# Fetching the sampled value blocks of sparse attention by SP's DMAs with register addresses, in place of GpSimd's indirect DMAs, for some of the sets

## The chip, the cores and the metric

The kernel runs on one core of one Trainium2 chip. The time is that of one execution on the device, in microseconds; the kernel before was timed three times, and the median counts. A profile of one further execution gives what every engine did and when.

## The reference

Block-sparse attention is followed by a feed-forward network. Attention has 4 batches, 8 heads, 768 positions and a head size of 64. Positions are grouped into 24 blocks of 32. A query block sees its neighbours, the first and the last block, and three sampled key blocks, which are an input and are the same for all batches and heads; the first and the last query block see everything.

```python
mask = np.abs(blk_i - blk_j) <= window          # window = 1
mask = mask | (blk_i == 0) | (blk_j == 0) | (blk_i == n_blocks - 1) | (blk_j == n_blocks - 1)
for qb in range(n_blocks):
    for kb in sampled_blocks[qb]:
        mask[qb*block:(qb+1)*block, kb*block:(kb+1)*block] = True
scores = np.where(mask, scores, -1e9)
attn = softmax(scores)
x = (attn @ v).transpose(0, 2, 1, 3).reshape(3072, 512)
h = x @ w_in                                     # 512 x 2048
g = np.maximum(h, 0.0) + np.log1p(np.exp(-np.abs(h)))
return g @ w_out                                 # 2048 x 512
```

The weights come as 64-bit floating point numbers, which the kernel turns into 32-bit ones itself.

## The kernel before

**Sets and units.** The 22 inner query blocks of a batch are taken four at a time: five groups of four and a last one of two. With the first and the last block, which see all keys and make a "whole" set of their own ahead of the last group, a batch has 7 sets, and the kernel 28: 0 to 4 are the groups of the first batch, 5 its whole set, 6 its last group of two blocks, 7 the first group of the next batch, and so on. A set is worked in two units of four heads each. A unit has scores (TensorE, L834), their masked minimum on VectorE (L840), exponents on ScalarE (L890), transposes on TensorE (L903) with a copy out of PSUM (L908, L910), and the product with the values (TensorE, L946; L960 for the whole sets, L933 for the last groups). After both units the set is normalised (L973 to L975), turned (L989) and put into the FFN's input (L1004, L1008). Units run as a pipeline: `pieces(n)` emits the scores of unit n + 2, the transposes of unit n + 1 and the products of unit n.

**Keys and values of a set.** Each of the four query blocks has eight key blocks: three neighbours, the first, three sampled, the last. The keys of the whole batch lie in SBUF; sampled ones are copied within SBUF by GpSimd (L715), at an address that comes from a register. The registers are loaded from a small packed table `pk` (L656), in which one 32-bit word holds the three samples of two query blocks, five bits each; `pack_blocks` makes it on VectorE (L579 to L585). The values are fetched from HBM for every set, into one of two buffers (`vbuf[m % 2]`, tile vg): the neighbours by one DMA from SP of 96 rows for each block (L755), first and last block by SP too (L764, L767), and the sampled ones by GpSimd's indirect DMA, one for each query block (L773), which fetches 96 rows of 2 KB after a column of row numbers in the table `ix`. `make_index` computes `ix` on VectorE for all four batches (L588 to L598). The buffer of set m + 2 comes free when the products of set m are done; `load_values(m + 2)` stands right behind them.

**What sets the order.** SP's instructions run in the order in which the program issues them: besides the value loads these are queries (`load_queries`, L649), key blocks of the next batch (L633), raw weights (L159) and converted weights on their way to HBM (L212), attention results (L1011) and output (L506, L512, L523). An instruction that waits holds back all behind it. GpSimd's indirect DMAs and key copies are kept in two lists, `value_work` and `key_work`, and `gather()` takes one of each after every piece of attention; `gathered(work, m)` empties a list up to set m before what needs it. GpSimd also does one step of the weight conversion (L193) and, in the second half, additions of the FFN (L337, L471). VectorE's order at the start is written out by hand: index, packed table, mask, key copies of set 0 (the `manual_schedule` block near L1079).

**Around it.** While the first sets run, TensorE has nothing else to do; a row of warm-up matmuls (L1077) stands ahead. From about 69 us on the FFN's matmuls (L268 to L270, L495 to L497) are mixed in. Attention ends at about 432 us, and the rest is FFN.

Of the kernel before, what the change touches and what calls it, by code (L numbers as in the profile page):

```python
# [8 lines left out]
F32 = mybir.dt.float32  # L9
# [10 lines left out]
BLOCK = 32  # L20
# [22 lines left out]
START = 4  # L43

SPREAD = 2

PARK = 8

# [9 lines left out]
def sparse_attention_ffn(  # L58
# [22 lines left out]
    nc = tc.nc  # L81
    B, NG, P, NP, NI, _ = q.shape
    NB = k.shape[2]
    S = NB * BLOCK
    LAST = NB - 1
# [7 lines left out]
    NR = 3  # L93
# [438 lines left out]
    ac = actx.enter_context(tc.tile_pool(name="ac", bufs=1, side="right"))  # L532
# [3 lines left out]
    blk = ac.tile([P, NB * NR * 2], I32, name="blk")  # L536
    rf = ac.tile([P, NB, NR], F32, name="rf")
# [3 lines left out]
    io = ac.tile([NR * BLOCK, 1], I32, name="io")  # L541
    first = ac.tile([P, 1], I32, name="first")
    iof = ac.tile([NR * BLOCK, 1], F32, name="iof")
    ixf = ac.tile([NR * BLOCK, NB], F32, name="ixf")
    ix = ac.tile([NR * BLOCK, B, NB], I32, name="ix")
    mask = ac.tile([P, NG, NS], F32, name="mask")
    iu = ac.tile([P, NG], I32, name="iu")
# [12 lines left out]
    for rows in (slice(0, NR * BLOCK), slice(NR * BLOCK, P)):  # L560
# [4 lines left out]
        out=vbuf[0][:, 0, 0, :], out_offset=None, in_=v,  # L565
# [11 lines left out]
    def pack_blocks():  # L577

        nc.vector.scalar_tensor_tensor(  # L579
            out=pkf, in0=rf[0:1, :, 1], scalar=32.0, in1=rf[0:1, :, 0], op0=ALU.mult, op1=ALU.add  # L580
        )
        nc.vector.scalar_tensor_tensor(
            out=pkf, in0=rf[0:1, :, 2], scalar=1024.0, in1=pkf, op0=ALU.mult, op1=ALU.add
        )
        nc.vector.tensor_copy(out=pk, in_=pkf[:, 1 : NB - 1])  # L585

    def make_index():
        nc.vector.tensor_copy(out=iof, in_=io)  # L588
        nc.vector.tensor_copy(out=rf, in_=blk.rearrange("p (i s w) -> p i s w", s=NR, w=2)[:, :, :, 0])

        for s in range(NR):
            rows = slice(s * BLOCK, (s + 1) * BLOCK)
            nc.vector.tensor_scalar(
                out=ixf[rows], in0=rf[rows, :, s], scalar1=float(BLOCK), scalar2=iof[rows, 0:1],
                op0=ALU.mult, op1=ALU.add,
            )
        for b in range(B):
            nc.vector.tensor_scalar_add(out=ix[:, b], in0=ixf, scalar1=float(b * S))  # L598

    def make_mask():  # L600
        nc.vector.tensor_copy(out=iuf, in_=iu)
# [36 lines left out]
    def overlapping(src, lo, n, rows):  # L638

        at = src[lo : lo + rows]  # L640
        pattern = [list(x) for x in at.ap]
        return bass.AP(at.tensor, at.offset, [pattern[0], [BLOCK * pattern[0][0], n], pattern[1]])

    def load_queries(m):
        if m >= len(order):
            return
        b, g = order[m]
        qc[b, g] = wk.tile([P, NP, NI, BLOCK], F32, tag="qc", name=f"qc{b}_{g}", bufs=2)
        nc.sync.dma_start(out=qc[b, g], in_=q[b, g])  # L649
# [3 lines left out]
    def registers(eng, us):  # L653
        for u in us:
            if (eng, u) not in regs:
                regs[eng, u] = eng.value_load(pk32[0:1, u : u + 1], min_val=0, max_val=(1 << 31) - 1)  # L656
        return [regs[eng, u] for u in us]
# [9 lines left out]
    def gathered(work, m):  # L667
        while work and work[0][0] <= m:
            work.pop(0)[1]()

    wanted = []

    def load_keys(*ms):

        wanted.extend(m for m in ms if m < len(order))
        while wanted and order[wanted[0]][0] in kT:
            gather_keys(wanted.pop(0))

    def end_keys(m, copies):

        for copy, slot, blkno in zip(copies, (NR, 2 * NR + 1), (0, LAST)):
            ins = copy(
                out=kg[m % 2][:, :, slot, :],
                in_=kT[order[m][0]][:, blkno : blkno + 1, :].to_broadcast([P, NI, NP * BLOCK]),
            )
            if m >= NG:
                tc.keep_in_program_order(ins)

    def gather_keys(m):
        b, g = order[m]  # L690
        ni = NI if g < NG - 1 else 2
        kd = kg[m % 2]

        def of_block(i):

            eng = (nc.vector if i < 2 else nc.scalar) if m == 0 else nc.gpsimd
            copy = nc.scalar.copy if m == 0 and i >= 2 else eng.tensor_copy
            if i == 0:
                at = kT[b][:, 4 * g : 4 * g + NR, :]
                pattern = [list(x) for x in at.ap]  # L700
                ins = nc.vector.tensor_copy(
                    out=kd[:, 0:ni, 0:NR, :].rearrange("p i s f -> p i (s f)"),
                    in_=bass.AP(at.tensor, at.offset, [pattern[0], [NP * BLOCK, ni], [1, NR * NP * BLOCK]]),
                )
                tc.keep_in_program_order(ins)
            if m % NG < 2 and i == (m >= NG):
                first = nc.vector.tensor_copy if m == 0 else nc.scalar.copy
                end_keys(m, (first, nc.scalar.copy))
            (r,) = registers(eng, [2 * g + i // 2])
            for s in range(NR):  # L710
                x = nc.s_assert_within(
                    eng.snap((r >> (16 * (i % 2) + 5 * s)) & 31), 0, LAST,
                    skip_runtime_bounds_check_because="a sampled block is one of the key blocks",
                )
                copy(  # L715
                    out=kd[:, i, 1 + NR + s, :], in_=kT[b][:, bass.ds(x, 1), :].rearrange("p n f -> p (n f)")
                )

        if g == 0 and b > 0:
            key_work.extend((m, lambda: None) for _ in range(ARRIVAL))  # L720
        key_work.extend((m, lambda i=i: of_block(i)) for i in range(ni))


# [15 lines left out]
    def load_values(m):  # L739
        if m >= len(sets):  # L740
            return
        b, g, whole = sets[m]
        vd = vg[sets[m]] = vbuf[m % 2]
        if whole:
            rows = vd.rearrange("p c i f -> p (c i) f")
            for n in range(0, NCH, 2):
                lo = b * S + n * P
                nc.sync.dma_start(
                    out=rows[:, n : n + 2], in_=v[lo : lo + 2 * P].rearrange("(t p) f -> p t f", p=P)
                )  # L750
            return
        ni = NI if g < NG - 1 else 2

        i0 = 1 if m == 0 else 0
        nc.sync.dma_start(  # L755
            out=vd[0 : 3 * BLOCK, 0, i0:ni], in_=overlapping(v, b * S + (4 * g + i0) * BLOCK, ni - i0, 3 * BLOCK)
        )
        if g < 2:

            for c, lo in enumerate((b * S, (b + 1) * S - BLOCK)):  # L760
                i1 = i0 if c == 0 else 0
                if m < SPREAD:
                    if i1 == 0:
                        nc.sync.dma_start(out=vd[3 * BLOCK : P, c, 0], in_=v[lo : lo + BLOCK])  # L764
                    spread.append((vd[3 * BLOCK : P, c, 0:1], vd[3 * BLOCK : P, c, 1:]))
                    continue
                nc.sync.dma_start(  # L767
                    out=vd[3 * BLOCK : P, c, i1:],
                    in_=v[lo : lo + BLOCK].unsqueeze(1).to_broadcast([BLOCK, NI - i1, DM]),
                )  # L770

        def of_block(i):
            nc.gpsimd.indirect_dma_start(  # L773
                out=vd[0 : 3 * BLOCK, 1, i, :],
                out_offset=None,
                in_=v,
                in_offset=bass.IndirectOffsetOnAxis(ap=ix[:, b, 4 * g + 1 + i : 4 * g + 2 + i], axis=0),
            )

        value_work.extend((m, lambda i=i: of_block(i)) for i in range(ni))  # L780


# [230 lines left out]
    def pieces(n):  # L1013
# [24 lines left out]
        def value_piece():  # L1038
            if n + 2 < len(units):
                exponents(n + 2)  # L1040
            if ended[1] is not None:
                turn(ended[1])
            if n < len(units):
                values(n)
                if ended[2] is not None:
                    load_values(ended[2] + 2)
            if scored is not None:
                load_queries(scored + 2)
# [27 lines left out]
    for n in range(WARM):  # L1076
        nc.tensor.matmul(warm[:, n % 4], ident, ident, start=True, stop=True)  # L1077
    with tc.manual_schedule(engines={mybir.EngineType.DVE}):
        make_index()  # L1079
        pack_blocks()  # L1080
        make_mask()
        load_keys(0)
        gathered(key_work, 0)
    load_queries(1)
    load_values(0)
    load_keys(1)
    scores(0)
    nc.vector.tensor_copy(out=mask[2 * BLOCK : P, NG - 1], in_=mask[0 : 2 * BLOCK, NG - 1])
    with tc.manual_schedule(engines={mybir.EngineType.Pool}):
        gathered(value_work, 0)  # L1090
        gathered(key_work, 1)
    spread_ends()
    load_values(1)
    load_keys(2)
    scores(1)
# [145 lines left out]
```

## Time and profile before

| | |
|---|---|
| median of three timed runs | 805.41 us (805.35 to 809.15) |
| profiled execution, its own time | 807.66 us |
| its span, first to last instruction | 805.6 us |
| TensorE busy | 767.6 us (95%) |
| VectorE, ScalarE, GpSimd busy | 597.4, 563.4, 397.2 us |
| mean granted TensorE clock | 0.979 |
| indirect DMAs (L773) | 88, 87.9 us of GpSimd, 998 ns on average |
| value loads from SP (L755, L764, L767, L748) | 24, 3, 12 and 12 |

The profile names engines PE (TensorE matmul), PEld (its weight loads), DVE (VectorE), ACT (ScalarE), POOL (GpSimd) and SP (SyncE); an added q is the engine's own queue of small instructions and DMA issues. A row of a timeline reads: start, duration, engine, line, operation, output tile <- input tiles, shape, number of instructions merged; in square brackets the idle time of the engine just before, and what ended it ("issue": nothing that the profile shows). A row of waits reads: who waited for whom, total time, number of waits, the longest. A row with a slash-separated triple gives the shortest, median and longest duration in ns.

### The profile page before, as it was taken

The numbers are of one execution on the slowest core, as the hardware profiler recorded it, in microseconds if no ns is written. First come the engines' busy times: TensorE is split into PE (matmuls) and PEld (weight loads), VectorE is DVE, ScalarE is ACT, GpSimd is POOL, SyncE is SP. The second block draws the span as 40 slices with busy tenths as digits, with TensorE's granted clock in tenths as the row PEclk, the third lists the DMA queues.
The fourth block names the chain that finished last, engine by engine and source line by source line (L and its number), as shares of the span: only waits on it lengthen the run. The fifth ranks groups of instructions, "written<-read, shape, count | busy, mean of one in ns | idle before, by whom it ended". The sixth has DMA issues, their size and how long they took to land.

```text
span 805.6 us, 21589 instructions
## 1 busy us (share of the span) xinstructions
PE 767.6 (95%) x8188; PEld 622.6 (77%) x8188; DVE 597.4 (74%) x1292; ACT 563.4 (70%) x1235; POOL 397.2 (49%) x617
## 2 busy tenths in 40 slices
PE   8688889999899999999999999999999999999997
PEld 8456657777677778777788878888998888988785
DVE  5667898887777777777655657888688797886654
ACT  4767877877687777777665767677776767766552
POOL 6663695543456426455100005425489597695400
PEclk9779998999999999999999999999999999999999
DMA  8669898678697786965714686221302315020021
GB/s 246 214 186 309 256 228 268 189 252 269 183 260 223 242 274 209 256 200 161 246 43 154 218 265 212 68 96 48 105 27 80 104 39 172 12 78 16 27 79 52
DMA packets 61175, 132.27 MB, mean 164 GB/s; under 512 B 5712, under 2 KB 18128, under 8 KB 60048
## 3 DMA queue, kind: packets, MB, share of 16 engines
q1 hardware_dynamic: 55072, 112.41, 44.6%
q0 software_dynamic: 5712, 17.57, 7.6%
q8 instruction: 64, 1.05, 0.6%
q10 hardware_dynamic: 288, 0.93, 0.3%
q14 instruction: 39, 0.32, 0.1%
HBM read 100.47 MB, written 30.41 MB: 162 GB/s over the span
## 4 chain that ended last, share of the span: by engine, by line
PE 55%; DVE 14%; ACT 14%; POOL 8%; issue 4%; DMA 2%; another core or an unknown queue 1%; POOLq 1%; SPq 0%; DVEq 0%; ACTq 0%
PE h L268 8%; PE h L269 7%; PE h L270 7%; PE o L495 5%; ACT pr L890 5%; PE o L496 5%; PE o L497 5%; PE t L903 3%; PE x L946 3%; POOL gq L337 3%; PE s L834 3%; DVE e L285 3%; POOL y L471 2%; PE acc L442 2%; PE acc L441 2%
## 5 line engine op out<-in xcount | busy, mean ns | idle before, releaser
L285 DVE SCALAR_TENSOR_TENSOR e<-u,e 128x512 f32<-128x512 f32 (+1 forms) x108 | 86.1, 797 | 94.4 <-ACT u L283 90.3
L337 POOL TENSOR_TENSOR gq<-gq 128x128 f32<-128x128 f32 x160 | 110.8, 715 | 63.1 <-DVE gq L322 60.0
L890 ACT ACTIVATE pr<-pr,nmax 128x256 f32<-128x256 f32 (+1 forms) x192 | 102.2, 534 | 33.1 <-DVE nmax L840 16.4
L773 POOL DMA_INDIRECT vg<-in_v_dram,ix x88 | 87.9, 998 | 69.8 <-PE x L946 38.3
L294 ACT ACTIVATE u<-u 128x512 f32<-128x512 f32 (+1 forms) x108 | 63.1, 584 | 71.7 <-DVE e L285 70.0
L715 POOL COPY kg<-kT 128x128 f32 x252 | 84.6, 380 | 52.0 <-PE s L834 43.2
L272 ACT ACTIVATE e<-h 128x512 f32<-128x512 f32 (+1 forms) x108 | 59.0, 547 | 57.5 <-PE h L270 57.1
L268 PE MATMUL h<-x,w 128*128 128x512 f32 x240 | 95.7, 399 | 2.4 <-ACT gh L275 1.0
L270 PE MATMUL h<-x,w 128*128 128x512 f32 x240 | 94.6, 394 | 0.0
L269 PE MATMUL h<-x,w 128*128 128x512 f32 x240 | 94.6, 394 | 0.0
L193 POOL TENSOR_TENSOR wt<-wt,raw 128x512 int32<-128x512 int32 x32 | 43.1, 1348 | 70.1 <-ACT raw L170 48.2
L283 ACT ACTIVATE u<-e 128x512 f32<-128x512 f32 (+1 forms) x108 | 63.1, 585 | 17.7 <-DVE gl L359 14.2
L840 DVE CUSTOM_DVE_ANT_1 pr<-s,mask 128x256 f32<-128x256 f32 x160 | 58.1, 417 | 23.3 <-PE s L834 10.4
L268 PE MATMUL h<-x,w1all 128*128 128x384 f32 x192 | 69.1, 360 | 3.4 <-DVE e L289 2.5
L903 PE MATMUL t<-ident,pr 128*128 128x128 f32 x448 | 65.6, 288 | 6.3 <-DVE x L1008 2.4
L270 PE MATMUL h<-x,w1all 128*128 128x384 f32 x192 | 65.2, 340 | 0.0
L269 PE MATMUL h<-x,w1all 128*128 128x384 f32 x192 | 65.2, 340 | 0.0
L277 ACT ACTIVATE e<-e 128x512 f32<-128x512 f32 (+1 forms) x108 | 63.0, 584 | 1.8
L903 PEld LDWEIGHTS t<-ident,pr 128*128 128x128 f32 x448 | 51.3, 145 | 14.1 <-issue 2.8
L946 PEld LDWEIGHTS x<-vg,pt 128*32 128x32 f32 x2560 | 42.8, 114 | 24.0 <-issue 22.4
L495 PE MATMUL o<-w1all,gh 128*128 128x512 f32 x144 | 61.3, 426 | 0.0
L946 PE MATMUL x<-vg,pt 128*32 128x64 f32 x2560 | 53.1, 228 | 7.6 <-issue 7.5
(141 smaller groups left out, 2049.4 us busy)
## 6 DMA issues: line engine op xcount, KB each, us to landing
vg<-in_v_dram SPq DMA_DIRECT2D x19, 768.0 KB
xD<-x SPq DMA_DIRECT2D x8, 1536.0 KB
raw<-in_w_in_dram SPq DMA_DIRECT2D x16, 512.0 KB
raw<-in_w_out_dram SPq DMA_DIRECT2D x16, 512.0 KB
qc<-in_q_dram SPq DMA_DIRECT2D x24, 256.0 KB
vg<-in_v_dram SPq DMA_DIRECT2D x12, 512.0 KB
yD<-os SPq DMA_DIRECT2D x24, 256.0 KB
x<-xD SPq DMA_DIRECT2D x4, 1536.0 KB
```

The costliest lines, as they stand in the source:

```text
L268: nc.tensor.matmul(ph, wh[:, cols], hi[:, c], start=(c == 0), stop=False)
L269: nc.tensor.matmul(ph, wh[:, cols], lo[:, c], start=False, stop=False)
L270: nc.tensor.matmul(ph, wl[:, cols], hi[:, c], start=False, stop=(c == NC - 1))
L283: nc.scalar.activation(u, e, AF.Copy, bias=1.0)
L285: nc.vector.scalar_tensor_tensor(out=e, in0=u, scalar=-1.0, in1=e, op0=ALU.add, op1=ALU.subtract)
L337: nc.gpsimd.tensor_tensor(out=a[:, to], in0=a[:, x], in1=a[:, y], op=op)
L495: nc.tensor.matmul(po[m], gh[:, cols], wh, start=first, stop=False)
L715: copy(out=kd[:, i, 1 + NR + s, :], in_=kT[b][:, bass.ds(x, 1), :].rearrange("p n f -> p (n f)"))
L773: nc.gpsimd.indirect_dma_start(out=vd[0 : 3 * BLOCK, 1, i, :], out_offset=None, in_=v, in_offset=bass.IndirectOffsetOnAxis(ap=ix[:, b, 4 * ...
L890: nc.scalar.activation(x, x, AF.Exp, bias=nmax[rows, r, j : j + 1], scale=-1.0, accum_out=rs[rows, h : h + 1])
L903: nc.tensor.transpose(ps[:, i, 0:rows], st["pr"][r][0:rows, c * P : (c + 1) * P], ident[0:rows, 0:rows])
L946: nc.tensor.matmul(xq[rows, h * D : (h + 1) * D], pt[r, 2 * j + c][:, rows], vd[:, c, i, h * D : (h + 1) * D], start=(c == 0), stop=(c == 1),)
```

## The change

For the sets in a new list, `BY_SP` = 1, 2, 3, 4 and every odd one from 5 to 27, the sampled values no longer come by GpSimd's indirect DMAs. SP issues, right after the neighbours and ends of the same set, one DMA for each query block and sample: 32 rows (64 KB), at an address that SP computes from a register with the packed samples. The whole sets among them (5, 19) have no sampled values. The other sets keep the indirect DMAs. At the start VectorE now reads the blocks, packs them, makes the index of the first batch and the mask, copies the keys of set 0, and adds the index of the later batches last.

```diff
+BY_SP = (1, 2, 3, 4, *range(5, 28, 2))
...
+    def read_blocks():
+        nc.vector.tensor_copy(out=rf, in_=blk.rearrange("p (i s w) -> p i s w", s=NR, w=2)[:, :, :, 0])
+
     def make_index():
         nc.vector.tensor_copy(out=iof, in_=io)
-        nc.vector.tensor_copy(out=rf, in_=blk.rearrange("p (i s w) -> p i s w", s=NR, w=2)[:, :, :, 0])
 
         for s in range(NR):
             rows = slice(s * BLOCK, (s + 1) * BLOCK)
             nc.vector.tensor_scalar(
-                out=ixf[rows], in0=rf[rows, :, s], scalar1=float(BLOCK), scalar2=iof[rows, 0:1],
+                out=ix[rows, 0], in0=rf[rows, :, s], scalar1=float(BLOCK), scalar2=iof[rows, 0:1],
                 op0=ALU.mult, op1=ALU.add,
             )
-        for b in range(B):
-            nc.vector.tensor_scalar_add(out=ix[:, b], in0=ixf, scalar1=float(b * S))
+
+    def index_of_later_batches():
+        for b in range(1, B):
+            nc.vector.tensor_scalar_add(out=ix[:, b], in0=ix[:, 0], scalar1=float(b * S))
...
+    def sampled(eng, g, i, s):
+        (r,) = registers(eng, [2 * g + i // 2])
+        return nc.s_assert_within(
+            eng.snap((r >> (16 * (i % 2) + 5 * s)) & 31), 0, LAST,
+            skip_runtime_bounds_check_because="a sampled block is one of the key blocks",
+        )
...
+        if m in BY_SP:
+            for i in range(ni):
+                for s in range(NR):
+                    x = sampled(nc.sync, g, i, s)
+                    nc.sync.dma_start(
+                        out=vd[s * BLOCK : (s + 1) * BLOCK, 1, i, :], in_=v[bass.ds(x * BLOCK + b * S, BLOCK)]
+                    )
+            return
         value_work.extend((m, lambda i=i: of_block(i)) for i in range(ni))
...
     with tc.manual_schedule(engines={mybir.EngineType.DVE}):
+        read_blocks()
+        pack_blocks()
         make_index()
-        pack_blocks()
         make_mask()
         load_keys(0)
         gathered(key_work, 0)
+        index_of_later_batches()
```

GpSimd's key copies (L715) now take their address from the same helper, with the same operations.

More of the change, by code (lines that the diff above doesn't have):

```diff
@@ L543, in sparse_attention_ffn @@
     iof = ac.tile([NR * BLOCK, 1], F32, name="iof")
-    ixf = ac.tile([NR * BLOCK, NB], F32, name="ixf")
     ix = ac.tile([NR * BLOCK, B, NB], I32, name="ix")
@@ L708, in of_block @@
                 end_keys(m, (first, nc.scalar.copy))
-            (r,) = registers(eng, [2 * g + i // 2])
+            registers(eng, [2 * g + i // 2])
             for s in range(NR):
[L711 to L714, printed above, removed]
+                x = sampled(eng, g, i, s)
                 copy(
```

## The prediction

> **What bounds the kernel now.** I read the table of stretches first, to see where TensorE is not full, then the timelines of TensorE and GpSimd inside the worst stretch, then the waits of ScalarE, then the rows that price what is moved.
>
> ```profile
> span 805.6 us, 21589 instructions
> ```
>
> ```profile
> core 0: us, PE busy (x) PEld busy (x) DVE busy (x) ACT busy (x) POOL busy (x), PEclk, DMA share, GB/s
> 16.00:70.00 54.00, 41.46 (x848) 27.32 (x833) 32.74 (x113) 37.21 (x103) 34.39 (x65) 0.81 0.77 223
> 24.00:34.60 10.60, 9.51 (x240) 6.42 (x239) 7.65 (x27) 10.55 (x29) 6.25 (x21) 0.81 0.54 181
> 54.00:60.00 6.00, 6.00 (x119) 4.04 (x125) 2.96 (x12) 4.18 (x12) 2.93 (x8) 0.60 0.19 49
> 70.00:120.00 50.00, 44.02 (x664) 31.07 (x666) 46.71 (x115) 41.69 (x101) 35.49 (x54) 1.00 0.87 256
> 120.00:420.00 300.00, 289.94 (x4416) 224.89 (x4416) 228.39 (x623) 222.96 (x575) 137.97 (x241) 0.98 0.73 220
> ```
>
> The columns are start and end, length, busy time of each engine with its instructions, granted clock, DMA share, rate. From 120 to 420 us TensorE is busy 290 of 300 us: GpSimd, half idle there, can give almost nothing. From 16 to 70 us no engine is full: TensorE 41.5, ScalarE 37.2, GpSimd 34.4 of 54 us, at a clock of 0.81. Nothing but the first sets of attention runs there, so what this stretch loses the whole kernel loses. The five sets whose values are needed in it are sets 0 to 4, and the change takes four of them (1 to 4) from GpSimd altogether.
>
> The loss has one face. In the value products (L946) of sets 1, 2 and 3, first half, TensorE stops again and again and waits for nothing that the profile shows. Set 2, and GpSimd at that time:
>
> ```profile
> 47.68 0.87 PE L946 MATMUL x<-vg,pt 128*32 128x64 f32 x47
> 48.75 0.26 PE L946 MATMUL x<-vg,pt 128*32 128x64 f32 x2 [0.20 <-issue]
> ...
> 52.41 0.46 PE L946 MATMUL x<-vg,pt 128*32 128x64 f32 x4 [0.40 <-issue]
> ```
>
> ```profile
> 48.16 0.93 POOL L773 DMA_INDIRECT vg<-in_v_dram,ix  x1 [0.16 <-issue]
> ...
> 52.52 0.94 POOL L773 DMA_INDIRECT vg<-in_v_dram,ix  x1 [0.16 <-issue]
> ```
>
> The 64 products last from 47.68 to 52.87, about as long as GpSimd issues the four indirect DMAs of set 3 (the first and the last stand here). They go to the other value buffer, so no data dependence joins the two. The other halves, and a unit of a later set without a gather beside it:
>
> ```profile
> 36.14 0.99 PE L946 MATMUL x<-vg,pt 128*32 128x64 f32 x33
> 39.02 1.05 PE L946 MATMUL x<-vg,pt 128*32 128x64 f32 x26 [0.29 <-issue]
> ...
> 61.38 0.42 PE L946 MATMUL x<-vg,pt 128*32 128x64 f32 x13
> 65.07 0.82 PE L946 MATMUL x<-vg,pt 128*32 128x64 f32 x35 [1.08 <-issue]
> ```
>
> ```profile
> 148.79 1.10 PE L946 MATMUL x<-vg,pt 128*32 128x64 f32 x64
> ```
>
> Undisturbed the unit takes 1.10 us. The same thing, I think, stands at the start, where the gathers of set 1 are issued: VectorE gets the scores of unit 1 only at 22.87 although TensorE issued the last of them by 17.91.
>
> ```profile
> 15.73 2.18 PE L834 MATMUL s<-kg,qc 64*32 64x256 f32 x64
> ```
>
> ```profile
> 16.96 0.94 POOL L773 DMA_INDIRECT vg<-in_v_dram,ix  x1 [0.15 <-issue]
> ...
> 20.64 0.92 POOL L773 DMA_INDIRECT vg<-in_v_dram,ix  x1 [0.30 <-issue]
> ```
>
> ```profile
> 18.30 0.08 DVE L840 DVE_READ_ACCUMULATOR2_ANT nmax<- 128x1 f32 x1
> 22.87 0.42 DVE L840 CUSTOM_DVE_ANT_1 pr<-s,mask 128x256 f32<-128x256 f32 x1 [4.48 <-remote]
> ```
>
> So my reading is: while GpSimd issues indirect DMAs in this crowded stretch, TensorE hardly moves, and ScalarE starves behind it. ScalarE's waits from 16 to 70 us:
>
> ```profile
> ACT pr L890 <- DVE nmax L840: 5.6, 3, 3.9
> ACT pt L910 <- PE t L903: 5.1, 4, 3.4
> ACT x L1004 <- remote: 3.9, 1, 3.9
> ACT x L1004 <- PE y L989: 1.8, 2, 1.3
> ```
>
> Together 16.4 us, nearly all of ScalarE's idle time (54 - 37.2 = 16.8). In 24 to 34.6 us, after set 1's gathers and before set 2's first, it is busy 10.55 of 10.6 us: without the stops it is the bound of this stretch.
>
> **What is removed.** 52 of the 88 indirect DMAs: four each of sets 1 to 4, 7, 9, 11, 15, 17, 21, 23 and 25, two each of 13 and 27 (5, 12, 19 and 26 are whole sets and have none). The stops they would take with them:
> - Start: 22.87 - 18.38 = 4.5 us.
> - Set 1's products: 40.07 - 36.14 - 1.10 = 2.8 us. Set 2's: 52.87 - 47.68 - 1.10 = 4.1. Set 3's: 65.89 - 61.38 - 1.10 = 3.4.
> - The cold clock that follows set 2's: 54 to 60 us is solid TensorE work at a clock of 0.60, which at full clock would be 3.6 us (2.4).
>
> Sum 17.2 us. Not all is to be had, since ScalarE and others are late next. ScalarE's 37.21 us of work leave at most 16.8. In 70 to 120 us, which is crowded too, it reaches 41.69 / 50 = 0.83; at that share the stretch takes 37.21 / 0.834 = 44.6 us, and 9.4 us are gained. I take 9.4: it is the row of the ordinary mixture, while the full 10.6 us lacked the gathers but also most of the loads. Ends: 0 (the stops have another cause) and 16.8.
>
> Later, 120 to 420 us, TensorE idles 10 us in all; the few gathers that still meet products could give 1 us (0 to 3).
>
> **What is added.** 156 DMAs on SP, three of 32 rows for each block. Nearest rows:
>
> ```profile
> L773 POOL DMA_INDIRECT vg<-in_v_dram,ix x88: 907/926/1465, 7.8 to 410.2; - x88
> L764 SPq DMA_DIRECT2D vg<-in_v_dram x3: 321/322/696, 2.7 to 10.4; - x3
> L755 SPq DMA_DIRECT2D vg<-in_v_dram x24: 328/331/1144, 2.1 to 408.7; - x24
> L715 POOLq ALU_OP x462: 4/35/698, 9.1 to 378.4; - x154
> ```
>
> L764 moves 32 rows from SP, the same shape at a fixed address: 0.32 us. The address of a key copy costs GpSimd's queue about three small operations of 35 ns: 0.1 us. So 0.42 us at least; with the slowest issue of L755 (1.14) 1.24 at most. I take 0.55, near the row of the same shape: 12 x 0.55 = 6.6 us of SP a set, against 4 x 0.93 of GpSimd. SP reads each packed word into a register once.
>
> Who waits for that? Behind the 12 in SP's order stand the query load (L649), the weight loads (L159), the weight parks (L212) and the output and key loads. SP's own record:
>
> ```profile
> 6.20 4.55 SPq L764 DMA_DIRECT2D vg<-in_v_dram  x2
> 22.90 0.35 SPq L649 DMA_DIRECT2D qc<-in_q_dram  x1
> ...
> 33.05 0.34 SPq L755 DMA_DIRECT2D vg<-in_v_dram  x1
> ```
>
> Set 1's twelve fit between 10.75 and 22.90, where SP waits anyway: free, and if that cover is gone the queries of the third group come up to 6.6 us later. Set 2's follow L755 at 33.05; they are issued by 33.05 + 0.38 + 6.6 = 40.0, and its products start at 47.68, in the shortened stretch some 2.5 us sooner. That leaves about 5 us for landing:
>
> ```profile
> 0.77 5.59 DMA blk<-in_blocks_dram
> ```
>
> A 72 KB load took 5.6 us at its worst, among the first loads. Lateness is then between nothing and 0.6 us a set for three sets; I count 1 us (0 to 2). From 120 us on about two thirds of the 28 sets share 300 us, some 15 us each, and only every second one is SP's, so it is hidden.
>
> The bytes are the same (12 x 64 KB for 4 x 192 KB), so DMA time in itself is costed at nothing; but loads come closer together, and 70 to 120 us has a DMA share of 0.87 and VectorE 46.7 of 50. I count 0.5 us given back (0 to 3).
>
> **VectorE at the start.** Packing moves ahead of the index, three of the four index additions go behind the key copies. One of the three packing operations:
>
> ```profile
> 7.70 0.17 DVE L579 SCALAR_TENSOR_TENSOR pkf<-rf 1x24 f32<-1x24 f32 x1
> ```
>
> Set 0's gathers start later by three of them, some 0.5 us, and the mask earlier. TensorE does its warm-up until the scores at 15.73, which covers both: nothing. If the cover were gone it would be 0.5 us.
>
> **Sum.** 9.4 + 1 - 1 - 0.5 = 8.9 us. Span 805.6 - 8.9 = 796.7; that execution took 807.66 us, 2.06 more than its span, so it would take 798.8. The median of the three timed runs, 805.41, is 2.25 below 807.66: predicted 796.5 us. For this kernel 0.5% (4 us) is about what a measurement can tell from no change.
>
> **Rival 1: the stops are not the gathers'.** The gathers of a set are issued when TensorE frees a buffer, and SP's large load (L755) starts on the same event; the stops may be owed to that traffic, or to instruction supply, which also shows as "issue". Then only GpSimd time goes (52 x 0.93 = 48 us of an engine with a third of its time free), worth 0 to 2 us: 804.5. For it: no visible semaphore joins the two. Against it: at 148.79 the products run in 1.10 us, in a stretch with a DMA share of 0.73, and set 2's stops last past 51 us, until the last gather at 52.5. The Trainium skill speaks for this rival: SBUF — State Buffer, section "SBUF: two separate sides", says that engine and DMA ports cannot slow each other and that TensorE never waits on another engine's port. By it the four stops would have to stay, and the time would be 804.5; the rows at 48 us agree badly with it.
>
> **Rival 2, slower: SP's queue.** If each of the 12 costs 1.24 us, set 2's values are issued 0.38 + 14.9 us after 33.05 and land up to 5.6 us later, 20.9 us against the 14.6 that the old course leaves: 6.3 us late, for sets 2, 3 and 4 18.9 us, less 9.4 gained, 9.5 us slower: 815. It decides from about (14.6 + 9.4 / 3 - 0.38 - 5.6) / 12 = 0.98 us a DMA. For it: some issues took over 1 us, and an SP issue can wait for the landing of an earlier load (L764 stood still until 10.4). Against: the medians of 0.32 and 0.33.
>
> **How the numbers follow.** My forecast has 0.69, its own range 788.6 (16.8 us gained) to 802. Rival 1 has 0.18, between 803 and 806; rival 2 has 0.13, 807 to 817. Faster by over 0.5% (under 801.4) takes the forecast except 0.03 of it and 0.01 of rival 1: 0.67. Within 0.5%: 0.19. Slower: 0.14. The range 788 to 806 holds the forecast and rival 1 and leaves out rival 2 and a rest.
>
> **What would show it.** Right: in the early units of sets 1 to 3 all 64 products run without "issue" stops, in about 1.1 us; the second unit's scores reach VectorE before 20 us; no half clock from 52 to 59 us; the first FFN matmul some 9 us earlier; ScalarE over 0.8 busy from 16 us on. Rival 1: the stops stand, without gathers beside them. Rival 2: products of sets 2 to 4 waiting for a value DMA, with SP's issues close behind one another up to that point. I am wrong altogether if the first 70 us shrink and the end does not move: then the work from 70 to 120 us gave it back.

## The result and the profile after

The kernel after takes 816.25 us (median of 4 runs, 812.42 to 817.01) against 805.38 us (4 runs, 804.11 to 809.15): a ratio of 1.0113, with a 95% interval of 1.0077 to 1.0149. It is slower by about 11 us, where 796.5 was predicted and 806 was the upper end of the range. Rival 2, SP's queue, had 815 us. The profiled execution took 816.86 us. Ratios here and below leave disturbed runs out and are not quotients of the medians, so the two can differ a little. Lines below 600 are shifted by two, the later ones by some five to seventeen: the products are L963 now, the gathers L782, SP's new DMAs L793, its large load L764 (L755 before), queries L654, weights L161.

The table of stretches (start and end, length, busy time of PE, PEld, DVE, ACT and POOL with their instructions, granted clock, DMA share, rate):

```profile
span 814.9 us, 22380 instructions
```

```profile
core 0: us, PE busy (x) PEld busy (x) DVE busy (x) ACT busy (x) POOL busy (x), PEclk, DMA share, GB/s
16.00:70.00 54.00, 38.29 (x824) 25.18 (x809) 34.59 (x117) 38.33 (x107) 21.13 (x53) 0.87 0.72 192
...
70.00:120.00 50.00, 41.89 (x635) 30.98 (x633) 44.87 (x109) 41.30 (x98) 30.27 (x48) 1.00 0.86 252
120.00:420.00 300.00, 284.26 (x4321) 214.64 (x4321) 222.33 (x612) 215.21 (x558) 110.43 (x211) 0.99 0.76 225
```

From 16 to 70 us GpSimd has lost 13 of its 34 us, as meant, but ScalarE is as idle as before (38.33 of 54 us; 0.71 where 0.83 was forecast), and fewer bytes move (192 GB/s against 223). From 120 to 420 us TensorE idles 15.7 us, 5.7 more than before. The first FFN product starts at 69.2 us (69.4 before). So the early stretch gained nothing, and the 11 us were lost after it.

TensorE's timeline says what became of the stops:

```profile
35.59 1.10 PE L963 MATMUL x<-vg,pt 128*32 128x64 f32 x64
...
58.40 0.39 PE L963 MATMUL x<-vg,pt 128*32 128x64 f32 x2 [1.71 <-DMA vg<-in_v_dram]
60.45 1.28 PE L963 MATMUL x<-vg,pt 128*32 128x64 f32 x36 [1.67 <-DMA vg<-in_v_dram]
```

Set 1's products, which had taken 3.9 us in pieces, run in 1.10 us: that stop is gone. Set 3's now stand still for something that the profile does name, a value DMA. The waits of the stretch from 16 to 70 us add the other late load:

```profile
PE x L963 <- DMA vg<-in_v_dram: 3.4, 2, 1.7
...
ACT wt L168 <- DMA raw<-in_w_in_dram: 2.9, 1, 2.9
```

SP's own timeline shows where these loads were:

```profile
13.40 13.50 SPq L793 DMA_DIRECT2D vg<-in_v_dram  x12
27.01 0.37 SPq L654 DMA_DIRECT2D qc<-in_q_dram  x1
...
31.76 12.02 SPq L793 DMA_DIRECT2D vg<-in_v_dram  x12
43.84 0.41 SPq L654 DMA_DIRECT2D qc<-in_q_dram  x1
44.30 0.42 SPq L161 DMA_DIRECT2D raw<-in_w_in_dram  x1
...
46.59 12.11 SPq L793 DMA_DIRECT2D vg<-in_v_dram  x12
```

Twelve DMAs take SP 12 us and more, twice the 6.6 us that I had given them, and queries and weights stand behind. Set 1's do not end before 22.90: the third group's queries go out at 27.01. Yet a single one is cheap; this is the view of line L793 (operation, count, shortest, median and longest duration in ns):

```profile
L793 SPq ALU_OP  x286: 16/37/193, 11.8 to 424.2; - x143
L793 SPq FUSED_REGOPS  x156: 7/55/70, 12.7 to 424.3; - x156
L793 SPq MOVE vg<-in_v_dram x156: 18/29/37, 13.4 to 424.4; - x156
L793 SPq DMA_DIRECT2D vg<-in_v_dram x156: 16/316/1440, 13.4 to 424.5; - x156
```

A median of 316 ns times twelve is 3.8 us. The chain of work that ended last, from 28 to 70 us, shows the rest. Its rows are start, length, what:

```profile
30.47 10.29 DMA vg<-in_v_dram
40.78 0.32 SPq L793
...
41.44 0.32 SPq L793
...
42.16 0.32 SPq L793
...
43.84 0.41 SPq L654
...
44.30 0.42 SPq L161
...
45.31 9.94 DMA vg<-in_v_dram
55.27 0.32 SPq L793
...
58.38 1.93 DMA vg<-in_v_dram
...
60.45 1.28 PE x L963 x36
```

SP issues set 2's large load (L764, 768 KB) at 30.47 and then seven of the twelve. The eighth starts at 40.78, at the moment when the large load has landed (30.47 + 10.29 = 40.76). Then the others follow at 0.65 to 0.72 us from start to start, then queries and weights, then set 3's large load at 45.31, and the same again: 45.31 + 9.94 = 55.25, the eighth of the twelve at 55.27. So each DMA on SP waits until the DMA eight places before it has landed, and nothing behind it can pass. The trace's records say why: the DMAs that SP issues take eight completion semaphores in turn (101 to 106, 109 and 110), and the eighth of the twelve reuses the large load's, 103. That is how this program is compiled; no run here shows whether the chip would allow more. In SP's waits, those for value loads before the twelve are one row:

```profile
SPq L793 <- DMA vg<-in_v_dram: 19.0, 12, 5.0
```

The Trainium skill, page Perfetto Trace Analysis, section "DMA Instruction — HWDGE (DVE, Sync)", says that the reported start of such an instruction lies behind its wait for semaphores; the trace agrees, since the rows of L793 are short while twelve of them last 12.02 us. A queue's price is read from start to start, not from its bars.

### The profile page after: what moved, and what is told of

Same layout as the page of the kernel before. It is cut to its first block, busy times and chain, and to the rows that moved or that the text cites. A ratio compares the mean times of both kernels' runs of the same rounds, so it can differ in the third digit from the quotient of the medians.

```text
span 814.9 us, 22380 instructions
## 1 busy us (share of the span) xinstructions
PE 767.5 (94%) x8188; PEld 619.2 (76%) x8188; DVE 596.4 (73%) x1291; ACT 563.4 (69%) x1235; POOL 351.0 (43%) x565
## 4 chain that ended last, share of the span: by engine, by line
PE 58%; DVE 12%; ACT 12%; POOL 7%; DMA 5%; issue 3%; SPq 1%; ACTq 0%; another core or an unknown queue 0%; DVEq 0%; POOLq 0%
PE h L270 9%; PE h L272 8%; PE h L271 8%; PE o L497 5%; PE o L499 5%; PE o L498 5%; ACT pr L907 3%; PE t L920 3%; POOL gq L339 3%; PE s L851 3%; DMA vg<-in_v_dram 3%; PE x L963 3%; POOL y L473 2%; DVE e L287 2%; PE acc L444 2%
## 5 line engine op out<-in xcount | busy, mean ns | idle before, releaser
L724 POOL COPY kg<-kT 128x128 f32 x252 | 88.5, 397 | 78.9 <-PE s L851 67.6
L857 DVE CUSTOM_DVE_ANT_1 pr<-s,mask 128x256 f32<-128x256 f32 x160 | 58.2, 418 | 29.2 <-PE s L851 28.3
L270 PE MATMUL h<-x,w1all 128*128 128x384 f32 x192 | 68.1, 355 | 1.1 <-DVE x L1025 0.5
L920 PEld LDWEIGHTS t<-ident,pr 128*128 128x128 f32 x448 | 49.4, 142 | 23.9 <-issue 7.1
L963 PEld LDWEIGHTS x<-vg,pt 128*32 128x32 f32 x2560 | 42.9, 112 | 30.5 <-issue 22.1
L271 PE MATMUL h<-x,w1all 128*128 128x384 f32 x192 | 64.7, 337 | 0.0
L272 PE MATMUL h<-x,w1all 128*128 128x384 f32 x192 | 64.6, 337 | 0.0
L963 PE MATMUL x<-vg,pt 128*32 128x64 f32 x2560 | 54.7, 225 | 8.0 <-DMA vg<-in_v_dram 3.4
L497 PE MATMUL o<-w1all,gh 128*128 128x512 f32 x144 | 60.9, 423 | 0.0
L499 PE MATMUL o<-w1all,gl 128*128 128x512 f32 x144 | 58.4, 409 | 2.5 <-DVE gl L361 2.5
```

What stands on the lines that cost most here:

```text
L270: nc.tensor.matmul(ph, wh[:, cols], hi[:, c], start=(c == 0), stop=False)
L271: nc.tensor.matmul(ph, wh[:, cols], lo[:, c], start=False, stop=False)
L272: nc.tensor.matmul(ph, wl[:, cols], hi[:, c], start=False, stop=(c == NC - 1))
L497: nc.tensor.matmul(po[m], gh[:, cols], wh, start=first, stop=False)
L499: nc.tensor.matmul(po[m], gl[:, cols], wh, start=False, stop=last)
L724: copy(out=kd[:, i, 1 + NR + s, :], in_=kT[b][:, bass.ds(x, 1), :].rearrange("p n f -> p (n f)"))
```

## The experiments

Ratios are to the kernel before in the same group of runs. "First FFN" is the start of the first FFN product in the profile (69.4 us before, 69.2 after), "end" that of the last set's second unit of products (431.6 and 442.4). The kernels with a fixed address leave the sampling out: they fetch neighbouring blocks in place of the sampled ones.

### First group: the parts apart

At this point two theories stood: that SP's queue makes the loss, and that the compiler's changed order of TensorE's instructions does (in the order, 61 stretches of products before became 83 after).

**e1_order_only**: only VectorE's new order.

```diff
-BY_SP = (1, 2, 3, 4, *range(5, 28, 2))
+BY_SP = ()
```

> No set is fetched by SP; only VectorE's new order at the start remains. All theories: the same as before, 805 us (803 to 807). If it is slower by more than 3 us, the start carries part of the loss.

Measured: 792.18 us, ratio 1.0000 (0.9972 to 1.0028). The reordering costs nothing, as predicted.

**e2_early_only** and **e3_late_only**: the change on sets 1 to 4 alone, and on the later sets alone.

```diff
+BY_SP = (1, 2, 3, 4)                  # e2
+BY_SP = tuple(range(5, 28, 2))        # e3
```

> Sets 1 to 4 by SP, later sets by indirect DMA. Theory Q (SP's queue: each small DMA costs SP about 1 us, 0.65 of issue and the rest a wait for an earlier landing, so values and all that stands behind them come late): the gathers' stops are gone, but SP's delay eats it, so the first FFN matmul stays near 69 us; the delay of set 4 (about 3 to 5 us) remains, 805 to 810 us. Theory O (the compiler puts TensorE's instructions in another order, and that costs): the order is nearly that of before, so no loss, and the gain of my forecast shows: 796 to 800 us.

> Only every odd set from 7 on by SP, sets 1 to 4 by indirect DMA. Theory Q: late sets give 5 to 8 us of loss, 810 to 813 us, with value waits in sets 7, 9, 15, 21 and 23. Theory O: nearly the whole loss is here, 812 to 817 us, without visible waits for values. My forecast's view (hidden from 120 us on): 805.

Measured: e2 810.03 us, 1.0205 (1.0153 to 1.0257); e3 801.19 us, 1.0114 (1.0064 to 1.0164). Both parts lose. e2 has nearly the old order of TensorE's instructions (63 stretches of products), so its loss is not the order's. e3 has the changed one (82). The value waits that theory Q expected in e3 are not there: from 85 to 420 us no product waits more than 0.2 us for a value DMA, in e3 or in the change. The longest named wait of TensorE's matmuls there is that of transposes for VectorE's minimum (L857): 8.4 us in both, 0.9 in e1. Theory O had expected no visible waits for values here, but nearly the whole loss, and e2's loss speaks against that.

**e4_one_dma**: each of SP's sets by one DMA with a fixed address, 768 KB at once.

```diff
-            for i in range(ni):
-                for s in range(NR):
-                    x = sampled(nc.sync, g, i, s)
-                    nc.sync.dma_start(
-                        out=vd[s * BLOCK : (s + 1) * BLOCK, 1, i, :], in_=v[bass.ds(x * BLOCK + b * S, BLOCK)]
-                    )
+            nc.sync.dma_start(
+                out=vd[0 : 3 * BLOCK, 1, 0:ni], in_=overlapping(v, b * S + 4 * g * BLOCK, ni, 3 * BLOCK)
+            )
```

> The sets of the change take the same bytes by one DMA from SP at a fixed address (768 KB, neighbour rows in place of the sampled ones, so the sampling is left out). Theory Q: SP is free again and the gathers' stops in sets 1 to 3 are gone too: 794 to 799 us, the size of my forecast. Theory O: the order is nearly that of before, the same 794 to 799. If the stops were not the gathers' (rival 1): 803 to 806.

Measured: 787.38 us, 0.9934 (0.9911 to 0.9956). The same bytes on the same queue gain; twelve issues lose.

This group held a surprise. The kernel before took 792.84 us here (19 runs, 787.63 to 796.1), and between 804.6 and 806.7 us in every other group. e1 runs the same instructions on TensorE in the same order, with all gathers, but the stops are hardly there. Its products of sets 1 and 2 and, below, the gathers beside them:

```profile
33.35 1.10 PE L963 MATMUL x<-vg,pt 128*32 128x64 f32 x64
...
42.80 0.42 PE L963 MATMUL x<-vg,pt 128*32 128x64 f32 x14
43.77 0.97 PE L963 MATMUL x<-vg,pt 128*32 128x64 f32 x50 [0.55 <-DMA vg<-in_v_dram,ix]
```

```profile
33.20 0.91 POOL L782 DMA_INDIRECT vg<-in_v_dram,ix  x1 [0.30 <-PE s L851]
...
42.08 0.93 POOL L782 DMA_INDIRECT vg<-in_v_dram,ix  x1 [0.16 <-issue]
43.32 0.92 POOL L782 DMA_INDIRECT vg<-in_v_dram,ix  x1 [0.31 <-DVE wt L185]
```

A gather from 33.20 to 34.11 lies on 64 products that take the undisturbed 1.10 us. Its first FFN is at 58.8 us, 10.6 earlier than in the trace of before. So a gather alone does not stop TensorE. Something that differs between groups is needed as well, and what it is was not found. In this group there was little for the change to win, and e2 lost the most. This group and the fifth, where the kernel before takes 805.97 us, ran on a chip of the same number (2), so the number of the chip does not decide it.

### Second group: what of the twelve costs

The kernel before takes 806.71 us here (21 runs).

**e5_fixed_address**: all 156 DMAs, without the address work.

```diff
-                    x = sampled(nc.sync, g, i, s)
...
-  in_=v[bass.ds(x * BLOCK + b * S, BLOCK)]
+  in_=v[(4 * g + i + s) * BLOCK + b * S : (4 * g + i + s + 1) * BLOCK + b * S]
```

> The same 156 DMAs of 32 rows from SP, at fixed addresses: no register arithmetic (rows next to the block in place of the sampled ones). Theory Q: an issue takes about 0.37 us in place of 0.65, waits for earlier landings remain: half of the loss goes, 806 to 811 us. If the waits for landings are most of it: 812 to 815. Theory O: TensorE's order is as changed as in the full change, so 815 us again.

Measured: 810.4 us, 1.0041 (1.0014 to 1.0068). SP's waits for landings remain and grow (L792 is the same DMA here):

```profile
SPq L792 <- DMA vg<-in_v_dram: 38.9, 19, 5.7
```

It was 19.0 us in the change. Set 2's twelve still take 11.37 us, since most of what the address work saves in them is waited away. But the registers need not be loaded ahead of them either: from the large load to the queries behind the twelve it is 11.87 us (29.42 to 41.29), against 13.37 in the change (30.47 to 43.84). The first FFN is at 63.9, and nearly two thirds of the loss are gone (1.0041 against 1.0113), where theory Q expected half. So the address work is more than a side matter.

**e6_set1_only**: `BY_SP = (1,)`.

> Only set 1 by SP, whose twelve DMAs run while SP has nothing else; TensorE's order is that of before to the last instruction. Theory Q: the stop at the start goes (units 1 and 2 some 3 to 4 us sooner) and SP's queue costs about 3 us of it through the late queries and weights: 801 to 804 us. Theory O: 801 us, nothing lost.

Measured: 807.8 us, 1.0018 (0.9998 to 1.0039), above both expectations. Set 1's gathers are gone, and the queries stand behind its twelve and go out at 27.16: the two about balance.

**e7_one_dma_all**: as e4, for all sets from 1 on (`BY_SP = tuple(range(1, 28))`), so that no gathers stand after set 0.

> All sets but 0 take the bytes by one DMA from SP at a fixed address (sampling left out), so GpSimd issues indirect DMAs for set 0 alone. Theory Q: as with one DMA for the sets of the change, and a little better, 792 to 798 us: the whole price of the indirect DMAs in this kernel.

Measured: 790.8 us, 0.9808 (0.9776 to 0.9839); first FFN at 60.9, end at 413.9, 17.7 us earlier than in the trace of before. That is what is gained when the values of all these sets come by one issue each, without the sampling.

**e8_pe_order**: the whole change with attention's matmuls and transposes kept in the program's order.

```diff
-nc.tensor.matmul(...)
+tc.keep_in_program_order(nc.tensor.matmul(...))
```

> The full change with TensorE's attention instructions held in the order in which the program writes them, as they nearly stood before. Theory Q: no better, 813 to 820 us, since waiting for late values now also holds back what was moved ahead. Theory O: back to 797 to 806 us.

Measured: 813.92 us, 1.0074 (1.0042 to 1.0106), end at 439.4. The interval overlaps that of the whole change (1.0077 to 1.0149): the order may have a share, but most of the loss stays without it. The transposes' wait for the minimum stays too (7.2 us from 85 to 420 us), so it is not the order's alone. What makes the later sets lose was not traced further.

### Third group: the dose

The kernel before takes 805.67 us here (17 runs).

**e9_order_again**: e1 once more, as the kernel before with a profile in this group.

> Only VectorE's new order at the start, all values by GpSimd's indirect DMAs (as e1). It stands for the kernel before on this chip, and shows in a profile whether the stops of TensorE beside the gathers occur here: with them sets 1, 2 and 3 take 3 to 5 us for the first unit's products and the first FFN product comes after 63 us; without them 1 to 2 us each and 58 to 60 us. Either way the ratio to the kernel before is 1.000 (0.997 to 1.003).

Measured: 805.32 us, 0.9999 (0.9981 to 1.0018), first FFN at 68.9. The stops are here, where gathers run beside the products: set 1's first unit, which falls between two gathers this time, takes 1.36 us, set 2's 6.03 and set 3's 5.03. Set 2's, first and last piece:

```profile
45.82 1.30 PE L963 MATMUL x<-vg,pt 128*32 128x64 f32 x47
...
51.26 0.59 PE L963 MATMUL x<-vg,pt 128*32 128x64 f32 x10 [0.44 <-issue]
```

**e10_whole_again**: the whole change.

> The whole change, beside e9 on the same chip. If the change is worth what SP's queue costs less what the stops give back: where e9 shows the stops, a ratio of 1.005 to 1.015; where e9 shows none, 1.018 to 1.03 (the early sets alone gave 1.0205 and the later ones 1.0114 on a chip where the stops were nearly absent). Rival, that the loss has nothing to do with the stops: the ratio is 1.011 (1.008 to 1.015) either way.

Measured: 814.68 us, 1.0118 (1.0090 to 1.0145). The result repeats. Both expectations allowed this number, so it separates nothing.

**e11_values_first**: for SP's sets one large DMA with a fixed address first, and then the twelve with their address work, of 64 bytes each into a spare tile.

```diff
+            nc.sync.dma_start(
+                out=vd[0 : 3 * BLOCK, 1, 0:ni], in_=overlapping(v, b * S + 4 * g * BLOCK, ni, 3 * BLOCK)
+            )
...
-                        out=vd[s * BLOCK : (s + 1) * BLOCK, 1, i, :], in_=v[bass.ds(x * BLOCK + b * S, BLOCK)]
+                        out=tiny[0:1, i, s, :], in_=v[bass.ds(x * BLOCK + b * S, 1), 0:16]
```

> For the sets of SP one DMA with a fixed address brings all the bytes first, then the same twelve DMAs with their address work follow, of 64 bytes each into a spare tile: the sampling is left out, SP's occupation stays, and the values are no longer late. If the loss is that the values come late: the ratio is within 0.004 of the one-DMA kernel (0.981 to 0.995, about 0.02 under e10). If the loss is what stands behind the twelve in SP's queue (queries, weights): within 0.004 of e10. Between them, it is both, in the proportion read.

Measured: 824.36 us, 1.0239 (1.0214 to 1.0264), outside both expectations. From 16 to 120 us no product waits for a value DMA; weights and queries are waited for instead (first two rows), and SP stands for landings (third row, L797 being the twelve):

```profile
ACT wt L168 <- DMA raw<-in_w_in_dram: 5.0, 1, 5.0
PE s L855 <- DMA qc<-in_q_dram: 4.9, 2, 4.1
```

```profile
SPq L797 <- DMA vg<-in_v_dram: 51.7, 28, 5.9
```

So the loss doesn't need late values: what stands behind a blocked SP is enough. I had overlooked that two large loads at the head of a burst hold two DMAs of it, one after the other, which is probably why it is slower than the change itself; as a measure of the two shares it is therefore not clean.

**e12_half**: of each of SP's sets the first half of the blocks by SP (six DMAs), the others by indirect DMAs.

```diff
-            for i in range(ni):
+            for i in range(ni // 2):
...
-            return
-        value_work.extend((m, lambda i=i: of_block(i)) for i in range(ni))
+        value_work.extend((m, lambda i=i: of_block(i)) for i in range(ni // 2 if m in BY_SP else 0, ni))
```

> Half the dose, nothing left out: of each set that SP served only the first half of the blocks by SP (6 DMAs, about 4 to 6 us), the others by indirect DMAs (2 a set). If the loss grows with SP's time from the first DMA on: about half of e10's excess. If it needs SP's burst to pass the slack of a set (my sum put that at about 0.98 us a DMA times 12, so some 11 us): less than a quarter of it, and where the stops occur a small gain, 0.995 to 1.002.

Measured: 793.82 us, 0.9863 (0.9834 to 0.9891): by the medians 11.9 us faster than before and 20.9 faster than the change, better than either theory had it. Stretch from 16 to 70 us, then SP:

```profile
16.00:70.00 54.00, 42.47 (x969) 28.35 (x955) 43.03 (x141) 45.47 (x124) 31.15 (x62) 0.97 0.96 266
```

```profile
31.77 4.43 SPq L793 DMA_DIRECT2D vg<-in_v_dram  x6
36.25 0.41 SPq L654 DMA_DIRECT2D qc<-in_q_dram  x1
```

```profile
SPq L161 <- DMA vg<-in_v_dram: 9.5, 6, 3.2
SPq L793 <- DMA vg<-in_v_dram: 8.7, 4, 5.5
```

ScalarE is busy 45.47 of 54 us, 0.84, where the prediction had 0.83. First FFN at 60.8, 8.1 us before e9's, where it had "some 9". Six take 4.43 us and the queries go out at 36.25. Behind the large load come six DMAs, the queries, and only then the eighth, which is a weight load (L161): it takes over the largest share of the waiting, where it costs little.

### Fourth and fifth group: is it the count?

The kernel before takes 804.62 us (29 runs) for e13 to e16 and 805.97 us (11 runs) for e17 and e18.

**e13_half_again**: e12 unchanged.

> The half dose again: 0.983 to 0.990 if this chip shows the stops of TensorE in the kernel before (its time then is 804 to 808 us); if it does not (kernel before at some 793 us), 0.995 to 1.003, for then there is little to gain. Rival, that the gain has nothing to do with the stops: 0.983 to 0.990 on either chip.

Measured: 793.61 us, 0.9848 (0.9812 to 0.9883). It holds; but a group without stops did not come again, so whether the half gains there stays open.

**e14_half_early**: e12 with `BY_SP = (1, 2, 3, 4)`.

> Half the dose on sets 1 to 4 alone, all later values by indirect DMAs. If the gain is the early stops', the whole of it is there: within 0.003 of e13, and its first FFN product is as early. Rival, that the later sets give a part: more than 0.004 above e13.

Measured: 799.82 us, 0.9945 (0.9919 to 0.9972). The first FFN is as early as e13's (61.2 and 61.3 us), but the end is 4.8 us later (422.6 and 417.8). The rival holds: some 5 to 6 us of the gain (4.8 by the ends, 6.2 by the medians) come from the later sets, where the prediction counted 1.

**e15_three_quarters**: nine DMAs and one gather a set (`ni - 1` in place of `ni // 2`).

> Nine DMAs of SP and one indirect DMA for a set. With the load ahead of them ten in a burst, so two wait for a landing. If it is the burst over eight that costs: clearly worse than e13, by 0.006 to 0.02, since the waits begin. If the cost grows evenly with SP's time: half of the way from e13 to the whole change, about 0.999 on a chip with stops (0.0127 above e13). If the gathers that are left cause what is lost: better than e13.

Measured: 803.55 us, 0.9980 (0.9951 to 1.0008). The ratio alone fits both of the first two theories. The chain from 28 to 70 us does not:

```profile
30.07 9.48 DMA vg<-in_v_dram
...
42.06 12.96 DMA vg<-in_v_dram
```

Two landings of large loads are again the longest pieces of the chain. SP's record has the eighth of the nine at 39.56 (30.07 + 9.48 = 39.55) and, a set later, at 55.03 (42.06 + 12.96 = 55.02). In e12's chain between 28 and 60 us one landing is left, of 3.07 us. In this stretch, what sets nine apart from six is the eighth place.

**e16_six_double**: six DMAs of two neighbouring blocks each, at fixed addresses, and no gathers for these sets.

```diff
+            for i in range(0, ni, 2):
+                for s in range(NR):
+                    nc.sync.dma_start(
+                        out=vd[s * BLOCK : (s + 1) * BLOCK, 1, i : i + 2, :],
+                        in_=overlapping(v, b * S + (4 * g + i + s) * BLOCK, 2, BLOCK),
+                    )
```

> Six DMAs for a set, each of two neighbouring blocks at a fixed address, so all the bytes go by SP and none of the set's by GpSimd; the sampling is left out. If the number of issues decides: within 0.004 of e13 or below it. If the bytes in SP's queue decide: near the kernel with twelve fixed addresses, 1.000 to 1.008.

Measured: 800.74 us, 0.9957 (0.9932 to 0.9982), between the two expectations. Six issues with all the bytes are better than twelve (e5, 1.0014 to 1.0068) and worse than six with half of them. So the number of issues counts, but it isn't all; whether the rest is the bytes, or TensorE's order (77 stretches of products against e13's 65), was not followed up.

**e17_half_all**: e12 with `BY_SP = tuple(range(1, 28))`.

> Half the dose in every set from 1 on that samples, in place of every second from 5 on. If a burst of six is free wherever it stands: 0.978 to 0.985, below e13's 0.9848. If SP's time adds up over neighbouring sets: 0.987 to 1.000.

Measured: 796.05 us, 0.9891 (0.9869 to 0.9913): not better than every second set (e13, 0.9812 to 0.9883). The waits of L793 for landings are 18.4 us in 7 against 12.0 in 4: the second expectation holds. The order differs as well (79 stretches against 65), which was not taken apart.

**e18_quarter**: three DMAs and three gathers a set (`1` in place of `ni // 2`).

> Three DMAs of SP and three indirect DMAs for each set that e13 halves. If the gain is in step with the gathers taken away (13 instead of 26 beside the critical sets): about 0.992. If three gathers stop TensorE as well as four do: 0.996 to 1.000. If the gain comes with the first DMAs: 0.985, as e13.

Measured: 801.92 us, 0.9945 (0.9928 to 0.9963): a third to a half of the half dose's gain, between the first two expectations and inside neither. The early stretch alone is another matter: the first FFN is at 68.9, 63.5, 60.8 and 60.9 us with four, three, two and no gathers a set (e9, e18, e12, e7; single traces of several groups), so the first gather taken away gives most there, and the last two nothing. Set 2's first unit in e18 (three gathers beside it), e13 (two) and e7 (none), first and last piece:

```profile
44.31 0.86 PE L962 MATMUL x<-vg,pt 128*32 128x64 f32 x44
...
48.59 0.43 PE L962 MATMUL x<-vg,pt 128*32 128x64 f32 x12 [0.50 <-issue]
```

```profile
42.73 0.77 PE L962 MATMUL x<-vg,pt 128*32 128x64 f32 x40
...
45.41 0.58 PE L962 MATMUL x<-vg,pt 128*32 128x64 f32 x21 [0.51 <-issue]
```

```profile
43.15 1.10 PE L960 MATMUL x<-vg,pt 128*32 128x64 f32 x64
```

From first start to last end: 4.71, 3.26 and 1.10 us, and 6.03 in e9 with four. That is 1.1 to 1.2 us for each gather in this unit. The trace of before has less: 1.0 for set 2 (5.19 us in all) and 0.9 for set 3 (4.51).

The whole curve, 0, 3, 6, 9 and 12 DMAs a set: 1.000, 0.9945, 0.985 to 0.986, 0.998, 1.012. At first the gathers leave, then SP's burst passes eight. The compiler's order changes along the way (61, 62, 65, 75 and 83 stretches of products), and only e8 tells the two apart.

## Why the prediction was wrong

**The stops and their worth: right in size.** In the groups where they occur, the products' stops grow with the gathers beside them. With all gathers behind set 0 gone (e7) the early stretch is as forecast nearly to the number: ScalarE is busy 44.30 of 54 us, 0.82 where the prediction had 0.83, and the first FFN comes 8.5 us earlier than in the trace of before, where it had some 9. Rival 1's price of 0 to 2 us falls there, but not every cause that it named, since a stop without a named wait also comes without gathers. In e7, whose last gather is issued at 12.0 us, TensorE stands between two scores:

```profile
50.33 1.08 PE L848 MATMUL s<-kg,qc 64*32 64x256 f32 x8 [3.20 <-issue]
```

The Trainium skill, page SBUF — State Buffer, section "SBUF: two separate sides", which speaks of ports, says that TensorE never waits at SBUF for a DMA or another engine; nothing here shows that the stops come from a port, and e1 shows gathers without stops. Their cause stays open; instruction supply, which rival 1 named, was not tested.

**The step that failed, the price of SP's twelve: "I take 0.55 ... 12 x 0.55 = 6.6 us of SP a set".** Set 2's twelve took 12.02 us, 1.00 a DMA, just past the 0.98 from which rival 2 was to decide. Of the 5.4 us that were missing, 12 x (0.65 - 0.55) = 1.2 are the issue itself, which I had nearly right. The other 4.2 are waits for landings, above all that of the set's own large load, eight places ahead. Another 0.95 us passed between the large load's issue and the first of them (30.81 to 31.76), where SP loads its registers. The prediction had seen a wait for a landing (L764 standing still until 10.4) and quoted it under rival 2, but its price for a set was twelve times a duration; no bar of the trace of before holds a wait that only a longer burst would meet. This step took the early gain away; the one on the later sets, below, turned it into a loss.

**"Set 1's twelve fit between 10.75 and 22.90: free": wrong.** They began at 13.40 and ended at 26.90. The queries left 4.1 us later (27.01 against 22.90), inside the 6.6 us that the prediction named as the price if the cover were gone. e6 shows that this eats the gain of set 1's gathers.

**"Lateness between nothing and 0.6 us a set": wrong.** Product and weight waits of 3.4 and 2.9 us replaced the stops, along one chain from SP to set 3's products. Counting only the values was a mistake by itself: e11 loses although its values are never waited for.

**"From 120 us on ... it is hidden", and 1 us gained there: wrong.** TensorE idled 5.7 us more there and 2.1 more from 70 to 120 us, and the last products ended 10.8 us later (442.4 against 431.6) though the first FFN product had come no later: this is where the 11 us were lost. A later set's twelve take 8.3 to 12.0 us in the trace after, and e3 loses 1.1% by the later sets alone. How the later bursts reach TensorE stays open: its products do not wait for values there. A part may be the order: e8, which keeps it, ends 3.0 us earlier than the change (439.4 and 442.4), though the intervals overlap. That the later gathers are worth taking away, e13 against e14 shows: 4.8 us by the ends.

**VectorE's order: nothing, as predicted** (e1, e9).

**Rival 2** had the place and the threshold, but not the reason: it was not that an issue costs 1.24 us. That its 815 lies near the measured time is luck. At the measured 1.00 us a DMA its own sum gives a set 0.38 + 12.0 + 5.6 - 14.6 = 3.4 us late, three sets 10.1 us, less 9.4: 0.7 us slower than before. The start came out so (69.2 against 69.4); the 11 us were lost after that, which rival 2 did not count. It had 0.13; the chance was read from medians of single issues.

## What to carry to other kernels

Price a burst of DMAs on a queue by its start-to-start time with the waits that the burst itself creates: count how many may be under way (here eight), find which transfer stands that many places ahead, and take its landing as the earliest time of the next issue. Then list what is queued behind the burst, not only what it fetches. When a swap of engines fails, try a part of it before dropping it: half the dose kept the gain, left the eighth place to a load that could wait, and ran 1.4 to 1.5% faster than before. Not tried, and next by this trace, is to issue the large load behind the small ones, so that no early DMA of the burst waits for it.

## What the runs showed of the hardware that was not expected

- Products of TensorE stood still for 0.9 to 1.2 us for each indirect DMA that GpSimd issued beside them (set 2's first unit: 6.03, 4.71, 3.26 and 1.10 us for four, three, two and none), without any wait that the profile names. Yet in e7 scores stood for 3.20 us in the same way with no gather beside them. In one group of runs the same gathers left the products at 1.10 us, and the kernel before was 12 us faster there (792.84 against some 805). What differs between the groups is not known.
- A DMA of 64 KB at an address from a register costs SP 0.65 us from start to start, of which the issue is 0.32; some four small operations (598 for 156 DMAs, medians of 29 to 55 ns) and their gaps are the rest.
- A 768 KB load with nine or twelve DMAs of 64 KB close behind it landed after 9.5 to 13.0 us (10.29 and 9.94 in the change, 9.48 and 12.96 with nine), and the DMA eight places behind it started within 0.03 us of that.
